# Attention and two mixing layers on one core: batch 0's queries and keys as whole tokens, and one table of priorities for all work

## The chip, the cores and the metric

The kernel runs on one core of a Trainium2 chip. The metric is the device time in microseconds of one execution; the median of three runs is given. A core has TensorE (PE in the profile; its weight loads are PEld), VectorE (DVE), ScalarE (ACT), GpSimd (POOL) and the queue that issues most transfers, SyncE (SP). Each engine works through its own instructions in the order in which they stand in its queue, and a semaphore holds an instruction until what it reads is there.

## The reference, cut to what matters

```python
B, H, S, D = 4, 8, 576, 64                     # queries, keys, values
scores = scale * q @ k^T                       # heads 0-3: the 32 keys up to the query
                                               # heads 4-7: every 4th key, 32 of them
attn = softmax(where(mask, scores, -1e9)); x = attn @ v      # -> (B, S, 512)
xk, xr = x_prev + mu_k * (x - x_prev), x_prev + mu_r * (x - x_prev)   # x_prev: the token before
kk = relu(xk @ w_k) ** 2                       # 512 -> 1024
x = sigmoid(xr @ w_r) * (kk @ w_v)             # MoE 1; 1024 -> 512
h = relu(x @ w_in); u, v = halves of h         # 512 -> 1024
x = (u * (w_spatial @ layernorm(v) + b)) @ w_out             # MoE 2
```

The weights arrive as float64, everything else as float32.

## The kernel before

**Products.** Every large product is made of two 12-bit parts of each operand (names end in `h` and `l`), hi·hi + hi·lo + lo·hi, so a product of 128 rows costs three matmuls of 288 or 512 columns. The parts of activations are made by a cast (ACT or DVE) and a subtraction of two SBUF tiles (DVE or POOL): `xh`/`xl` of the mixed tokens `xm`, `kh`/`kl` of the squared relu `kr`, `x2h`/`x2l` and `gh`/`gl` in MoE 2.

**Weights.** `split_weight` takes 512 float64 columns of 128 rows at a time (a chunk): a transfer into `room`, a scaled copy on ACT into `temps`, a shift and two two-input bit operations on DVE (TENSOR_SCALAR and two SCALAR_TENSOR_TENSOR on `temps`), then the cast to the high part (`wkh`, `wrh`, `wvh`) and the subtraction for the low part (`wkl`, `wrl`, `wvl`, on POOL or DVE). `w_k`, `w_r` and `w_v` are 20 chunks, all before batch 0's first half is through; `w_in` and `w_out` are 12 more (`raw`, `tmp`).

**Attention.** `att(b, qd)` does four heads of a batch: scores of blocks of 32 queries against windows of 64 keys (`psS`), softmax (`mx`, `sm` in the tile `st`, `pr`), transposes (`psT`, `pt`), values (`vw`), and the result into the batch's tokens `x`. Batches 1 to 3 get their queries and keys turned by DVE (`ld` to `qT`, `kT`). Batch 0 has tiles `nat` with 8 tokens to a partition, 72 partitions; TensorE transposes them in pieces of 72 by 128 (`nat_turn`), and ACT and DVE copy halves of 64 partitions into `qT` and `kT`, four copies a tile.

**Halves.** MoE 1 runs per half of a batch's tokens (288): `moe1_k` (products with `w_k`), `moe1_r` (`w_r`, sigmoid), `moe1_v` (`w_v`, and on DVE the gate `x<-psM,x`, four per half, the last step of a half). MoE 2 runs per batch after all of MoE 1.

**Order.** The kernel writes all steps into a `Plan` with what each reads and writes, estimated costs per engine, and a time at which it should stand; `schedule` is a list schedule that gives each step an engine and a place. `order` runs it with the written times as priorities, then twice with due times worked out backward from TensorE's order (`due`), and keeps the order whose estimated end is soonest. Where a step can run on several engines, it takes the one with the soonest estimated end, with a handicap `pen = {'dve': 792, 'pool': 22, 'act': 0}` for all steps alike. Where the plan sees TensorE idle early on, it puts in products of constants that nothing reads (`psT<-const` in the profile). Every planned instruction is recorded on one helper line (L299), so the rows below are told apart by their tiles.

Of the kernel before, what the change touches and what calls it, by code (L numbers as in the profile page):

```python
# [30 lines left out]
CH = 512  # weights converted at a time  # L31
NT = S // P  # full tiles of tokens
# [4 lines left out]
def blocks(dil):  # L37
    """a head's blocks: the first query and the first key of each, two by two, with tokens in
    the order of the head's residue classes; the last of a class repeats 16 queries of the
    one before"""  # L40
    if not dil:
        return [(QB * i, max(0, QB * (i - 1))) for i in range(S // QB)]
    q0, k0 = (0, 32, 64, 96, 112), (0, 0, 32, 64, 80)
    return [
        (CL * c + q0[s], CL * c + k0[s])
        for two, last in (((0, 1), (0, 2)), ((2, 3), (1, 3)))
        for c, s in [(c, s) for c in range(DIL) for s in two] + [(c, 4) for c in last]
    ]


class Plan:
    """Instructions as a program that names what it reads and writes, put in an order in which
    the engines wait little: a list schedule with estimated costs (in ns)."""
# [3 lines left out]
    def __init__(self):  # L57
        self.ops = []
        self.written = {}
        self.read = {}  # L60
        self.turn = {}
        self.groups = {}
        self.hot = {}
        self.end = {}
        self.slow = {}
        self.at = 0.0
# [5 lines left out]
    def add(self, cost, emit, r=(), w=(), table=None, lat=130, at=None, after=(), hot=1.0):  # L72
        i = len(self.ops)
        self.hot[i] = hot
# [19 lines left out]
    def schedule(self, prio):  # L94
        ops = self.ops
        pen = {'dve': 792, 'pool': 22, 'act': 0}
# [30 lines left out]

        def release(i):
            if not ops[i][0]:
                # a step that no engine takes  # L130
# [17 lines left out]
        while any(avail.values()):  # L148
            best = None
            for e, c in avail.items():  # L150
# [4 lines left out]
                for i in sorted((i for i in c if at[i] <= t0 + wide), key=lambda i: (prio[i], i)):  # L155
                    start = max(free[e], at[i])
                    end = start + ops[i][0][e]
                    # another engine that would end it sooner
                    if any(
                        max(free[f], at[i]) + k + pen.get(f, 0) < end + pen.get(e, 0)  # L160
# [8 lines left out]
            if best is None:  # L169
                # each engine leaves its first to another: take the soonest end  # L170
                best = min(
                    (max(free[e], at[i]) + ops[i][0][e], max(free[e], at[i]), i, e)
# [16 lines left out]
            end = start + cost[e] * slow  # L189
# [20 lines left out]
    def due(self, out):  # L210
        """the latest starts with which the tensor engine would never wait, in its order of out"""
        ops = self.ops
        late = [math.inf] * len(ops)
        t = 3000.0
        for _, i, e in out:
            if e == "pe":
                late[i] = t
                t += ops[i][0][e]
        for _, i, e in reversed(out):
            cost, _, deps, _, lat, at, _ = ops[i]  # L220
            if late[i] == math.inf:
                late[i] = 1e9 + at
            for d in deps:
                c = ops[d][0]
                lat = ops[d][4]
                k = min(c.values()) if c else 0
                if "dma" in c:
                    k, lat = c["dma"], 2000
                late[d] = min(late[d], late[i] - lat - k)
        return late  # L230

    def order(self):
        ops = self.ops
        prio = [o[5] for o in ops]
        best = self.schedule(prio) + (prio,)
        guess, out = best[:2]
        for _ in range(2):
            late = self.due(out)
            guess, out = self.schedule(late)
            if guess < best[0]:  # L240
                best = guess, out, late
        if guess > best[0]:
            self.schedule(best[2])
        self.out = best[1]
        # where the tensor engine would idle early on, products that nothing reads keep its clock up
# [24 lines left out]

def act(n):
# [19 lines left out]
class Ordered:  # L291
    """An engine whose instructions keep the order in which they are given."""
# [18 lines left out]
def kernel(  # L311
# [36 lines left out]
    # ---- pools; those of a phase are opened when the plan comes to it  # L348
# [18 lines left out]
    enter("pro", "nat")  # L367
# [4 lines left out]
    # ---- constants  # L372
# [3 lines left out]
    # which keys a block's queries see, a row of blocks: as dilated heads start, as others do  # L376
# [15 lines left out]
    # the room of later batches' tokens serves the conversion of weights first  # L392
# [5 lines left out]
    # ---- weights: float64 words from DRAM, as float32, split into two parts of 12 bits  # L398
    weights = {}

    def split_weight(pool_name, src, rows, cols, name, raw_of, nraw, tmp_of, ntmp, order, step=0, lead=0):
        s = src.bitcast(U32).rearrange("(r p) c -> p r c", p=P)

        def parts():
            if name not in weights:
                weights[name] = (
# [5 lines left out]
        base_at = plan.at  # L412
        for j, (c0, r) in enumerate((c0, r) for c0 in range(0, cols, CH) for r in range(rows)):
# [10 lines left out]
            def words(kr=kr):  # L424
# [3 lines left out]
            add({"dma": 1460}, load, w=[rk], r=order, lat=2000, at=plan.at - lead)  # L428
# [3 lines left out]
            add(  # L432
                {"act": act(CH)},
# [16 lines left out]
            def lower(e, kt=kt, words=words):  # L450
# [5 lines left out]
            add({"dve": dve2(CH)}, shift, r=[tk], w=[tk])  # L456
            add({"dve": dve(CH)}, upper, r=[tk, rk], w=[tk])
            add({"dve": dve(CH)}, lower, r=[tk, rk], w=[tk])
# [3 lines left out]
                r=[tk], w=[(key, 0)],  # L462
# [6 lines left out]
                r=[tk, (key, 0)], w=[(key, 1)],  # L469
            )  # L470

    def wkeys(name, r, c):
# [3 lines left out]
    # ---- batch 0's queries and keys come with 8 tokens to a partition  # L476
    NP = 72
    TP = S // NP
    apart = [0, 0]  # heads of a pair side by side
    nats = [  # L480
        [
            get("nat", [NP, TP, 2, D] if apart[g // 2] else [NP, 2, TP, D], F32, f"nat{x}{g}")
            for g in range(4)
        ]
# [3 lines left out]
    def nat_load(g, at):  # L488
        for x, src in enumerate((q, k)):
            if apart[g // 2]:  # L490
                for h in range(2):
                    dma(
                        820, nats[x][g][:, :, h],
                        src[0, 2 * g + h].rearrange("(i t) d -> i t d", i=NP),
                        w=[("nat", x, g, h)], at=at,
                    )
            else:
                dma(
                    820, nats[x][g],
                    src[0, 2 * g : 2 * g + 2].rearrange("h (i t) d -> i h t d", i=NP),  # L500
                    w=[("nat", x, g, h) for h in range(2)], at=at,
                )
# [971 lines left out]
```

## Time and profile before

| | |
|---|---|
| median of 3 runs | 620.29 us (619.29 to 623.86) |
| profiled execution, first to last instruction | 618.7 us |
| TensorE busy | 566.7 us, mean granted clock 0.958 |
| DVE busy | 309.5 us |
| ACT busy | 311.7 us |
| POOL busy | 274.0 us |

The profile's span is 1.6 us under the median, so what is added or taken in the span is added or taken from the median alike. Busy times are sums over the whole span; the stages differ a great deal, and a busy TensorE can be one that runs at half clock or that multiplies constants.

### The profile page before, as it was taken

The numbers are of one execution on the slowest core, as the hardware profiler recorded it, in microseconds if no ns is written. First come the engines' busy times: TensorE is split into PE (matmuls) and PEld (weight loads), VectorE is DVE, ScalarE is ACT, GpSimd is POOL, SyncE is SP. The second block draws the span as 40 slices with busy tenths as digits, with TensorE's granted clock in tenths as the row PEclk, the third lists the DMA queues.
The fourth block names the chain that finished last, engine by engine and source line by source line (L and its number), as shares of the span: only waits on it lengthen the run. The fifth ranks groups of instructions, "written<-read, shape, count | busy, mean of one in ns | idle before, by whom it ended". The sixth has DMA issues, their size and how long they took to land.

```text
span 618.7 us, 12888 instructions
## 1 busy us (share of the span) xinstructions
PE 566.7 (92%) x5233; PEld 523.4 (85%) x5234; DVE 309.5 (50%) x543; ACT 311.7 (50%) x721; POOL 274.0 (44%) x303
## 2 busy tenths in 40 slices
PE   6766967999799998998899999999999999999996
PEld 4655856889798988988899999987979988998995
DVE  2599999976526169189350500259613314223120
ACT  6575684586285478473453526057335234423321
POOL 3146766573454157166461515008803722551170
PEclk7789788999899999998899999999999999999999
DMA  8998948366123502223200000042010011001002
GB/s 167 184 205 207 226 128 194 79 111 121 22 63 64 116 2 70 88 68 98 78 2 1 2 0 24 1 122 69 1 69 1 1 58 28 1 17 52 2 1 85
DMA packets 91371, 43.75 MB, mean 71 GB/s; under 512 B 76672, under 2 KB 82864, under 8 KB 91312
## 3 DMA queue, kind: packets, MB, share of 16 engines
q1 hardware_dynamic: 90976, 42.09, 28.5%
q0 software_dynamic: 336, 0.84, 0.8%
q8 instruction: 41, 0.67, 0.5%
q14 instruction: 18, 0.15, 0.1%
HBM read 38.20 MB, written 4.72 MB: 69 GB/s over the span
## 4 chain that ended last, share of the span: by engine, by line
PE 61%; DVE 20%; DMA 8%; issue 3%; ACT 3%; POOL 2%; SPq 1%; DVEq 0%; ACTq 0%; POOLq 0%
PE psM L299 44%; PE psB L299 15%; DVE temps L299 4%; DVE tmp L299 3%; DVE xm L299 3%; DVE st L299 3%; PE psT L299 2%; DMA nat<-in_q_dram 2%; DMA room<-in_moe_w_k_dram 2%; DVE pr L299 1%; SPq L299 1%; DVE xl L299 1%; DMA ld<-in_q_dram 1%; POOL pr L299 1%; DMA room<-in_moe_w_r_dram 1%
## 5 line engine op out<-in xcount | busy, mean ns | idle before, releaser
L299 PE MATMUL psM<-kh,wvh 128*128 128x288 f32 x256 | 79.3, 310 | 5.8 <-DVE x L299 3.6
L299 PE MATMUL psM<-xh,wkh 128*128 128x288 f32 x256 | 79.0, 309 | 4.8 <-ACT xh L299 2.3
L299 PE MATMUL psM<-xl,wkh 128*128 128x288 f32 x256 | 78.0, 305 | 1.2 <-POOL xl L299 1.2
L299 PE MATMUL psM<-kh,wvl 128*128 128x288 f32 x256 | 77.1, 301 | 1.3 <-DVE wvl L299 1.1
L299 PE MATMUL psM<-xh,wkl 128*128 128x288 f32 x256 | 77.4, 302 | 0.0
L299 PE MATMUL psM<-kl,wvh 128*128 128x288 f32 x256 | 76.6, 299 | 0.0
L299 POOL TENSOR_TENSOR kl<-kr,kh 128x288 fp32r<-128x288 f32 x55 | 48.5, 884 | 62.5 <-ACT kh L299 61.8
L299 PEld LDWEIGHTS psM<-kh,wvh 128*128 128x128 f32 x256 | 49.7, 194 | 7.9 <-DVE x L299 4.1
L299 PEld LDWEIGHTS psM<-xh,wkh 128*128 128x128 f32 x256 | 50.1, 196 | 5.8 <-ACT xh L299 2.4
L299 POOL TENSOR_TENSOR pr<-pr,st 128x384 f32<-128x384 f32 (+1 forms) x35 | 33.9, 980 | 47.1 <-DVE st L299 45.1
L299 POOL TENSOR_TENSOR xl<-xm,xh 128x288 fp32r<-128x288 f32 x50 | 44.2, 892 | 21.6 <-ACT xh L299 21.4
L299 DVE SCALAR_TENSOR_TENSOR xm<-xd,mu,x 128x288 f32<-128x288 f32 x64 | 47.9, 761 | 9.8 <-POOL xl L299 9.6
L299 PEld LDWEIGHTS psM<-xl,wkh 128*128 128x128 f32 x256 | 50.1, 196 | 1.6 <-POOL xl L299 1.4
L299 PEld LDWEIGHTS psM<-kh,wvl 128*128 128x128 f32 x256 | 49.6, 194 | 1.8 <-DVE wvl L299 1.3
L299 PEld LDWEIGHTS psM<-xh,wkl 128*128 128x128 f32 x256 | 50.3, 197 | 0.0
L299 PEld LDWEIGHTS psM<-kl,wvh 128*128 128x128 f32 x256 | 49.7, 194 | 0.0
L299 ACT ACTIVATE kr<-psM 128x288 f32<-128x288 f32 x64 | 26.1, 408 | 39.9 <-PE psM L299 37.7
L299 PE MATMUL psM<-xh,wrh 128*128 128x288 f32 x128 | 39.6, 309 | 5.5 <-ACT kr L299 3.9
L299 POOL TENSOR_TENSOR vl<-vt,vh 128x512 fp32r<-128x512 f32 x13 | 17.2, 1323 | 52.2 <-ACT vh L299 41.1
L299 DVE TENSOR_TENSOR x<-psM,x 128x288 f32<-128x288 f32 x32 | 14.2, 452 | 52.0 <-PE psM L299 52.0
L299 PE MATMUL psM<-wsh,vh 128*128 128x288 f32 x128 | 38.3, 299 | 1.0 <-ACT u L299 0.5
L299 PE MATMUL psM<-xl,wrh 128*128 128x288 f32 x128 | 38.2, 298 | 0.8 <-POOL xl L299 0.8
(156 smaller groups left out, 1601.0 us busy)
## 6 DMA issues: line engine op xcount, KB each, us to landing
vw<-in_v_dram SPq DMA_DIRECT2D x45, 128.0 KB, 4.1
room<-in_moe_w_k_dram SPq DMA_DIRECT2D x8, 512.0 KB, 8.8
room<-in_moe_w_v_dram SPq DMA_DIRECT2D x8, 512.0 KB
raw<-in_moe_w_in_dram SPq DMA_DIRECT2D x8, 512.0 KB, 3.7
out_dram<-ot SPq DMA_DIRECT2D x16, 256.0 KB, 3.0
ld<-in_q_dram SPq DMA_DIRECT2D x48, 72.0 KB, 2.9
ld<-in_k_dram SPq DMA_DIRECT2D x48, 72.0 KB, 2.5
room<-in_moe_w_r_dram SPq DMA_DIRECT2D x4, 512.0 KB, 6.5
```

What stands on the lines that cost most here:

```text
L299: return self.tc.keep_in_program_order(getattr(self.engine, name)(*args, **kw))
```

## The change

**Batch 0's queries and keys.** The tiles `nat` become views of two large tiles `early0` (queries) and `early1` (keys) that stand where the two parts of `w_v` will stand (pool `w1`, tags `wv0`, `wv1`); the parts of `w_v` are written only after the step `wv room`, that is after all that reads the early tiles. Of heads 0 to 3 a pair comes as 128 partitions of 9 whole tokens, of heads 4 to 7 each head as 48 partitions of 12. `nat_turn` uses ordinary float32 products with the identity, one per token and head (64 by 64 or 48), 168 in all in place of 64 transposes, and two copies of 128 partitions a tile in place of four of 64. Values of heads 4 to 7 of batch 0 lie in the early tiles too, and all values of batch 0 are issued by SP, none by POOL. Two of three score chunks of batch 0 use a `psM` bank. The working tiles of MoE 1 (`mp`) no longer take the place of `nat`.

**Priorities.** `due` and the search for the best of three orders are gone. Each step's priority is its written time plus two numbers of a table `TUNE` (an offset and a slope over the group's steps), and each group has its own handicaps for DVE and POOL. Estimated costs are new (`pe`, `packets`, additions for ACT), and the schedule lets a two-input or wide DVE step and a POOL step slow each other (`begin`, `until`).

```diff
+TUNE = {
+    ('k', 0, 0): {'kh': (-1112, -2225, 400, 22), 'kl': (-5930, 4753, 1500, -800), 'kr': (9298, 2270, -200, 0), 'psM': (1385, 1749, 792, 22), 'xd': (998, -581, 0, 2000), 'xh': (-11122, 10184, 400, 22), 'xl': (-274, 6549, -200, 300), 'xm': (-15869, -4890, 792, 22)},
...
+            more, grow, dve_, pool_ = TUNE.get(g[0], {}).get(g[1], (0, 0, 792, 22))
+            prio.append(o[5] + more + grow * (k / count[g]))
+            self.pens.append({"dve": dve_, "pool": pool_})
...
-        pen = {'dve': 792, 'pool': 22, 'act': 0}
+        pens = self.pens
...
+        def until(e, i, t, c):
+            if e == "pool":
+                h, rate = held["dve"], 0.4
+            elif e == "dve" and two[i]:
+                h, rate = held["pool"], 0.35
+            else:
+                return t + c
+            if h <= t:
+                return t + c
+            return t + c / rate if c / rate <= h - t else h + c - (h - t) * rate
...
-        best = self.schedule(prio) + (prio,)
...
-        for _ in range(2):
-            late = self.due(out)
-            guess, out = self.schedule(late)
...
+        _, self.out = self.schedule(self.tuned())
...
+    early = [
+        pools["w1"].tile([P, NF * DM], F32, tag=f"wv{x}", name=f"early{x}") for x in range(2)
+    ]
...
-                for m in range(4):
-                    if apart[hp // 2]:
-                        i = t[:, 4 * b + m].rearrange("p h d -> p (h d)")
-                    else:
-                        i = t[:, b, 2 * m : 2 * m + 2].rearrange("p t d -> p (t d)")
-                    nc.tensor.transpose(ps[:, m * NP : (m + 1) * NP], i, ident[:NP, :NP])
...
+                for j, tok in enumerate(toks):
+                    for h in range(2):
+                        r = slice(h * D, h * D + m)
+                        nc.tensor.matmul(
+                            ps[h * D : (h + 1) * D, j * m : (j + 1) * m], t[r, tok], ident[r, r],
+                            start=True, stop=True,
+                        )
...
-                choice = {"dma": cost, "pool": 1100} if b == 0 else {"dma": cost}
...
+                dma(cost, o, i, w=[key], at=at1 - 1950 + 40 * qd if b == 0 else at1 - 472)
...
+            if b == 0 and ch != 1:
+
+                ps, skey = bank()
...
+    add({}, lambda e: None, w=["wv room"], after=users_of(early_keys), lat=0)
```

How this moves instructions shows best at three places.

**TensorE at the start**, before: between the turning of the second pair's keys (`nat11`) and the first scores stands the turning of the third pair's queries (`nat02`).

```order
L299 MATMUL psM1_95<-ident_76,nat11_88 128x72 x4
...
L299 MATMUL psM2_96<-ident_76,nat02_85 128x72 x4
L299 MATMUL psM0_94<-ident_76,nat02_85 128x72 x4
...
L299 LDWEIGHTS identb_77
L299 MATMUL psS0_100<-mask_79,identb_77 128x384
L299 MATMUL psS0_100<-kT0_93,qT0_92 32x64 x2
```

The same place after the change: the first scores (now in `psM2`) follow the second pair's keys (`early1`) with nothing but products of constants between, and the third pair's queries come after them.

```order
L436 MATMUL psM0_88<-ident_76,early1_84 64x64 x10
L436 MATMUL psM1_89<-ident_76,early1_84 64x64 x8
...
L436 LDWEIGHTS identb_77
L436 MATMUL psM2_90<-mask_79,identb_77 128x384
L436 MATMUL psM2_90<-kT0_87,qT0_86 32x64 x2
...
L436 MATMUL psM1_89<-ident_76,early0_83 64x48 x16
```

So the first scores no longer stand behind a tile of heads 4 and 5.

**SP's queue ahead of the first weights**, before (the first chunks of `w_k` are the `room` rows; POOL issues five more loads of values by itself):

```order
L299 DMA nat03_86<-in_q_dram 72x2x512
L299 DMA nat13_90<-in_k_dram 72x2x512
L299 DMA vw0_91<-in_v_dram 64x9x64
L299 DMA vw0_91<-in_v_dram 64x8x64
L299 DMA vw0_91<-in_v_dram 64x2x64
L299 DMA room1_80<-in_moe_w_k_dram 128x1024
L299 DMA room3_81<-in_moe_w_k_dram 128x1024
```

and after:

```order
L436 DMA early0_83<-in_q_dram 48x768 x2
L436 DMA vw0_85<-in_v_dram 64x9x64
L436 DMA vw0_85<-in_v_dram 64x8x64
L436 DMA vw0_85<-in_v_dram 64x9x64
L436 DMA room1_80<-in_moe_w_k_dram 128x1024
L436 DMA vw0_85<-in_v_dram 64x8x64
L436 DMA vw0_85<-in_v_dram 64x2x64
L436 DMA early1_84<-in_k_dram 48x768
L436 DMA room3_81<-in_moe_w_k_dram 128x1024
```

The first chunk moved ahead of the last pair's keys and of the values that POOL issued before; the second chunk stands behind four more loads.

**The low parts in batch 0's second half**, before, on POOL:

```order
L299 TENSOR_TENSOR kl1_922<-kr0_877,kh1_912 128x288
L299 TENSOR_TENSOR xd1_638<-x1_1349 128x288
L299 TENSOR_TENSOR kl2_948<-kr1_884,kh2_936 128x288
L299 TENSOR_TENSOR xd2_778<-x1_1349 128x288
L299 TENSOR_TENSOR xd3_810<-x1_1349 128x288
L299 TENSOR_TENSOR kl3_1000<-kr2_905,kh3_987 128x288
L299 TENSOR_TENSOR kl4_1022<-kr0_877,kh4_998 128x288
```

The same steps after the change stand on DVE:

```order
L436 TENSOR_TENSOR kl0_926<-kr2_914,kh0_903 128x288
L436 TENSOR_TENSOR kl1_946<-kr0_877,kh1_929 128x288
L436 TENSOR_TENSOR kl2_959<-kr1_908,kh2_934 128x288
L436 TENSOR_TENSOR kl3_971<-kr2_914,kh3_961 128x288
L436 TENSOR_TENSOR kl4_1030<-kr0_877,kh4_991 128x288
L436 TENSOR_TENSOR kl5_1071<-kr1_908,kh5_1018 128x288
L436 CAST xh2_821<-xm0_746 128x288
L436 TENSOR_TENSOR kl6_1105<-kr2_914,kh6_1093 128x288
L436 SCALAR_TENSOR_TENSOR xm0_746<-xd0_683,mu_78,x1_1432 128x288
```

All eight of this half moved to DVE, in front of the next batch's `xm`. Over the whole program `kl` goes from 55 on POOL and 9 on DVE to 19 and 45, `gl` from 30 and 2 to 0 and 32, and ACT gives 16 of 64 first relus, 16 of 58 casts to `xh` and 12 of 63 casts to `kh` to DVE.

## Rows read from the trace of the kernel before

**Rows 1.** The page: busy us and share of each engine; granted clock in 40 slices.

```profile
PE 566.7 (92%) x5233; PEld 523.4 (85%) x5234; DVE 309.5 (50%) x543; ACT 311.7 (50%) x721; POOL 274.0 (44%) x303
...
PEclk7789788999899999998899999999999999999999
```

**Rows 2.** Windows: width; busy of PE, PEld, DVE, ACT, POOL; clock; DMA share; GB/s.

```profile
0.00:30.00 30.00, 20.81 (x260) 15.64 (x260) 11.38 (x24) 18.89 (x54) 7.22 (x16) 0.72 0.90 177
30.00:120.00 90.00, 67.58 (x975) 59.12 (x974) 88.02 (x135) 57.38 (x128) 56.33 (x53) 0.89 0.77 177
120.00:300.00 180.00, 167.98 (x2020) 159.75 (x2018) 108.61 (x190) 108.28 (x243) 87.25 (x99) 0.98 0.33 76
300.00:400.00 100.00, 97.90 (x724) 97.39 (x724) 25.95 (x44) 43.21 (x111) 36.96 (x45) 0.98 0.04 11
400.00:440.00 40.00, 38.47 (x225) 34.19 (x224) 29.62 (x59) 23.30 (x52) 18.09 (x17) 0.96 0.25 74
440.00:600.00 160.00, 160.00 (x982) 146.44 (x981) 45.48 (x94) 56.52 (x128) 65.73 (x73) 1.00 0.06 22
```

**Rows 3.** The chain that ended last: shares by engine; its longest piece.

```profile
PE 61%; DVE 20%; DMA 8%; issue 3%; ACT 3%; POOL 2%; SPq 1%; DVEq 0%; ACTq 0%; POOLq 0%
...
302.52 93.12 PE psM L299 x690
```

**Rows 4.** Timeline of the first 30 us: start, us, what, and what ended idling.

```profile
6.03 9.29 SPq L299 DMA_DIRECT2D vw<-in_v_dram  x3
...
12.71 2.03 ACT L299 COPY kT<-psM 64x288 f32<-64x288 f32 x3
15.37 1.23 SPq L299 DMA_DIRECT2D room<-in_moe_w_k_dram  x2
...
16.36 1.19 PE L299 MATMUL psM<-ident,nat 72*128 72x72 f32 x8 [3.05 <-DMA nat<-in_q_dram]
...
18.37 1.51 PE L299 MATMUL psS<-kT,qT 64*32 64x64 f32 x48
...
25.27 0.67 ACT L299 ACTIVATE temps<-room 128x512 f32<-128x512 f32 x1 [0.81 <-DMA room<-in_moe_w_k_dram]
```

**Rows 5.** Groups of DVE from 30 to 120 us: busy us, mean ns of one.

```profile
L299 DVE SCALAR_TENSOR_TENSOR temps<-room,temps 128x512 uint32<-128x512 uint32 x38 | 37.1, 995 | 0.0
L299 DVE TENSOR_SCALAR temps<-temps 128x512 uint32<-128x512 uint32 x19 | 13.0, 692 | 0.9 <-ACT temps L299 0.9
L299 DVE SCALAR_TENSOR_TENSOR xm<-xd,mu,x 128x288 f32<-128x288 f32 x12 | 10.4, 883 | 0.0
L299 DVE TENSOR_TENSOR xl<-xm,xh 128x288 fp32r<-128x288 f32 x3 | 2.7, 901 | 0.0
```

**Rows 6.** The tiles temps, kl: duration ns min/median/max; single DVE steps while POOL is idle.

```profile
L299 DVE SCALAR_TENSOR_TENSOR temps<-room,temps x40: 641/765/1775, 27.2 to 110.8; 128x512 uint32<-128x512 uint32 x40
L299 DVE TENSOR_SCALAR temps<-temps x20: 385/421/1515, 26.0 to 108.7; 128x512 uint32<-128x512 uint32 x20
...
L299 POOL TENSOR_TENSOR kl<-kr,kh x55: 797/809/1267, 67.4 to 378.7; 128x288 fp32r<-128x288 f32 x55
L299 DVE TENSOR_TENSOR kl<-kr,kh x9: 448/902/1541, 78.6 to 375.5; 128x288 fp32r<-128x288 f32 x9
...
27.20 0.68 DVE L299 SCALAR_TENSOR_TENSOR temps<-room,temps 128x512 uint32<-128x512 uint32 x1
...
117.03 0.50 DVE L299 SCALAR_TENSOR_TENSOR xm<-xd,mu,x 128x288 f32<-128x288 f32 x1
```

**Rows 7.** Timeline of DVE: the 4th and the 20th of the 32 gates.

```profile
120.43 0.41 DVE L299 TENSOR_TENSOR x<-psM,x 128x288 f32<-128x288 f32 x1
...
299.47 0.45 DVE L299 TENSOR_TENSOR x<-psM,x 128x288 f32<-128x288 f32 x1
```

**Rows 8.** Waits, whole span (DVE) and 120 to 320 us (PE): total us, times, longest.

```profile
DVE kl L299 <- ACT kh L299: 56.9, 5, 13.1
...
PE psM L299 <- DVE x L299: 4.2, 2, 3.6
PE psT L299 <- POOL pr L299: 2.1, 5, 1.0
```

**Rows 9.** Timeline of ACT: attention's last results of batch 0; the first cast of w_v.

```profile
58.62 0.67 ACT L299 COPY x<-psT 128x256 f32<-128x256 f32 x2
...
90.85 0.62 ACT L299 CAST wvh<-temps 128x512 fp32r<-128x512 f32 x1
```

More of the change, by code (lines that the diff above doesn't have):

```diff
@@ L65, in __init__ @@
         self.slow = {}
+        self.two = []
+        self.tags = []
+        self.tag = ("start",)
         self.at = 0.0
@@ L70, in slot, with add @@
         return self.turn[name]
-    def add(self, cost, emit, r=(), w=(), table=None, lat=130, at=None, after=(), hot=1.0):
+    def add(self, cost, emit, r=(), w=(), table=None, lat=130, at=None, after=(), hot=1.0, two=False):
         i = len(self.ops)
+        self.two.append(two)
+        self.tags.append(self.tag)
         self.hot[i] = hot
@@ L126, in schedule, with begin @@
         out = []
+        held = {"dve": 0.0, "pool": 0.0}
+        two = self.two
+        def begin(e, i):
+            t = max(free[e], at[i])
+            if e == "dve" and two[i] == "both":
+                t = max(t, held["pool"])
+            return t
+        def until(e, i, t, c):
[8 more added lines that the diff above has]
+            return t + c / rate if c / rate <= h - t else h + c - (h - t) * rate
         def release(i):
@@ L188, in schedule @@
                 table[0] = tab
-            end = start + cost[e] * slow
+            end = until(e, i, start, cost[e] * slow)
+            if e == "pool" or e == "dve" and two[i]:
+                held[e] = end
             for f in cost:
@@ L268, in order, with pe, packets @@
         return res
+def pe(n, cols):
+    return n * (4.7 + cols * 0.442)
+def packets(n, size):
+    took = {128: 13, 256: 23, 512: 30, 1024: 58, 1920: 125, 2048: 112, 2304: 133, 3072: 165, 4096: 219}
+    return n * took[size] / 16
 def act(n):
@@ L399, with split_weight @@
     weights = {}
-    def split_weight(pool_name, src, rows, cols, name, raw_of, nraw, tmp_of, ntmp, order, step=0, lead=0):
+    def split_weight(pool_name, src, rows, cols, name, raw_of, nraw, tmp_of, ntmp, order, step=0, lead=0, room=()):
         s = src.bitcast(U32).rearrange("(r p) c -> p r c", p=P)
@@ L405, in parts @@
             if name not in weights:
+                if name == "wv":
+                    weights[name] = tuple(
+                        pools[pool_name].tile([P, rows, cols], F32R, tag=f"wv{x}", name=f"wv{x}")
+                        for x in range(2)
+                    )
+                    return weights[name]
                 weights[name] = (
@@ L474, in wkeys, with spread, cut @@
         return [((name, r, c0), 0), ((name, r, c0), 1)]
-    NP = 72
-    TP = S // NP
-    apart = [0, 0]
+    def spread(hp):
+        return 9 if hp < 2 else 12
+    NATS = sum(spread(g) for g in range(4)) * D
+    VW = 2 * 10 * D
+    early = [
+        pools["w1"].tile([P, NF * DM], F32, tag=f"wv{x}", name=f"early{x}") for x in range(2)
+    ]
+    def cut(t, n, c0):
+        return t[:, c0 : c0 + n * D].rearrange("p (t d) -> p t d", d=D)
     nats = [
[L481 to L484, printed above, removed]
+        [cut(early[x], spread(g), D * sum(spread(i) for i in range(g))) for g in range(4)]
         for x in range(2)
@@ L550 @@
+            w_ = len(toks) * m
+            add(
+                {"act": actp(w_) + 147, "dve": dve(w_) + 100}, keep, r=[pkey],
+                w=[key + (2 * b,), key + (2 * b + 1,)],
+            )
     NQK = 3
@@ L740, in att @@
                     ),
-                    r=[s_key, ("mx", pk)], w=[("pr", pk)],
+                    r=[s_key, ("mx", pk)], w=[("pr", pk)], two=not pe_mask,
                 )
@@ L1039, in users_of @@
         return res
-    def open_mp(e):
-        stacks["pro"].close()
-        enter("one", "mp", reuse_waits="tile")
-    add({}, open_mp, w=["mp"], after=users_of([("nat", x, g, h) for x in range(2) for g in range(4) for h in range(2)]), lat=0)
+    plan.at = 1391
+    plan.tag = ("wv room",)
+    add({}, lambda e: None, w=["wv room"], after=users_of(early_keys), lat=0)
+    split_weight("w1", w_v, NF, DM, "wv", lambda i: raws[i], raw1, lambda i: tmps[i], tmp1, [], 51, 480, ["wv room"])
+    plan.at = 600
+    plan.tag = ("start",)
+    fresh_x(1, [("raw", 0), ("raw", 2)])
+    fresh_x(2, [("tmp", i) for i in range(4)])
+    fresh_x(3, [("raw", 1), ("raw", 3)])
     gap = [361, 786, 488]
@@ L1369, in moe2 @@
                 lambda e, eg=eg, g=g: copy(e, eg()[:, :, b % 2], f32(g()[:, :, NT * P :])),
-                r=[(nm, c, 1) for c in range(NC)], w=[("e" + nm, b % 2)],
+                r=[(nm, c, 1) for c in range(NC)], w=[("e" + nm, b % 2)], two="both",
             )
```

268 lines of the change are left out of this document (146 added, 122 removed), and 84 rows, old and new, of the table TUNE.

## The prediction, on record before the run

> **What bounds the kernel now.** I read the page first, then the busy times by stretch, then the chain of waits, then single rows in the stretches where TensorE stands. The page shows TensorE busy for 92% of the span [rows 1]. That number misleads early on. In the first 120 us TensorE is busy 20.8 + 67.6 = 88.4 us, but at granted clocks of 0.72 and 0.89 (a mean between the full level and the half one), and part of that multiplies constants [rows 2]. From 440 to 600 us it is busy 160.00 of 160.00 at full clock: nothing that the change does to other engines can shorten that. The chain's longest piece, 93.12 us for 690 products, is 135 ns a product and ends at 395.6 [rows 3]; it is bound by TensorE alone.
>
> So the time to be won lies ahead of 440 us. From 0 to 30 us the transfers run at a share of 0.90 and 177 GB/s, and DVE is busy 11.38 us [rows 2]. From 30 to 120 us DVE is busy 88.02 of 90.00 us: this is the stage of the 20 weight chunks, and DVE sets its pace. From 120 to 300 us TensorE idles 180.00 - 167.98 = 12.0 us and loses another 180 x (1 - 0.98) = 3.6 us to the clock; from 300 to 440 us it idles 2.1 + 1.5 us and loses 2.0 + 1.6 us to the clock [rows 2]. Beyond 120 us that is 15.6 + 7.2 = 22.8 us in all, the most that better order can return there.
>
> **The start.** The first scores run at 18.37 us. The last copy of the second pair's keys ended at 12.71 + 2.03 = 14.74 us, but the turning of `nat02`, which stands before the scores, waited 3.05 us for its transfer and ran at 16.36 [rows 4]. After the change that tile stands behind the scores. Ahead of them are four tiles of 0.295 MB and the mask, 1.43 MB; at 177 GB/s that is 8.1 us, with about 1 us to the first issue 9 us, and with turning and two copies (0.7 us a copy at the pace of the `kT` row, 2.03 / 3) 11 to 12 us. If the tiles come no sooner, the end of the copies still bounds it: 14.7 us. So the scores come 3.7 to 7 us earlier; I take 6. The first chunk of `w_k` was converted from 25.27 us on [rows 4]. Ahead of it and with it stood 0.5 + 2.9 MB on SP and 0.7 MB on POOL, 4.1 MB, 23 us at that rate, which agrees. Now it is 3.3 MB: 18.4 + 1 us, 5 to 6 us earlier. Both inputs of DVE's long queue therefore come some 6 us earlier. The copies themselves fall from four of 64 partitions to two of 128 a tile, which frees ACT for the 18 exponentials of the first block. Turning takes 168 products in place of 64 transposes: 24 products (48 records) of scores took 1.51 us, 63 ns each, so 10.6 us, against 8 transposes in 1.19 us, 149 ns each, 9.5 us [rows 4]. TensorE has that 1 us to spare there. If it had none, it would cost 1 us. I take **-6 us** for the start; ends -3 and -8.
>
> **The new wait.** The casts of `w_v` must now wait until batch 0's attention is through. Its last results of that kind started at 58.62 us, the first cast of `w_v` at 90.85 [rows 9]: 32 us of cover. I cost it at nothing; if attention came later than that, ACT's later casts, and behind them `temps`, would stand for the excess.
>
> **30 to 120 us.** The order of the changed kernel has, in DVE's queue up to the fourth gate, more work: 8 more low parts of weights at 0.68 us, two more steps each of `xd`, `pr`, `mx` and `pt`, fewer `xm`. With the durations that these steps have while POOL is idle (0.68 us for two-input steps of 512, 0.50 for `xm`, 0.45 for differences of 288, 0.42 for the shift) [rows 6] the queue adds up to 86.0 us before and 95.2 after, +9.2. But POOL has 35 steps there in place of 57, 31 us in place of 53 by its own group means. What POOL costs DVE shows in the same stretch: 38 x (995 - 680) + 19 x (692 - 421) + 12 x (883 - 500) + 3 x (901 - 450) ns = 12.0 + 5.1 + 4.6 + 1.4 = 23.1 us lost [rows 5, 6] beside 56.33 us of busy POOL [rows 2], 0.41 us of DVE for each us of POOL. So 22 us less POOL returns 9.1 us. The sum is **0**; ends -5 and +5, since a single two-input step loses anything from nothing to 1.1 us (641 to 1775 ns) [rows 6].
>
> **120 to 300 us.** From the 4th gate (120.43) to the 20th (299.47) [rows 7] DVE's queue grows by 35.5 us at those durations (95.4 to 130.9: 24 more `kl` at 0.45, 14 squares, 13 `xd`, some 12 casts each to `xh` and `kh`), and POOL's falls by 30 us, which returns 12. Net +23 us, in a stretch in which DVE idles 180.00 - 108.61 = 71 us [rows 2]. It fits, and each step is done sooner: a `kl` takes 0.81 us on POOL and 0.45 on DVE alone [rows 6]. TensorE's waits there are for gates, low parts and softmax steps of POOL [rows 8]. I take half of the 15.6 us: **-8 us**; ends 0 and -13, and above 0 in a rival below. **300 to 440 us**, where `w_in` and the change to MoE 2 stand, I take **-3** of 7.2; ends +2 and -5. **After 440 us**: 0, by the full row.
>
> The sum: 618.7 - 6 + 0 - 8 - 3 = 601.7 us of span. The span stands 1.6 us under the median of 620.29, so **603 us**. The best ends make 618.7 - 8 - 5 - 13 - 5 + 1.6 = 589.
>
> **A rule that would give more.** Rows 5 and 6 show a two-input DVE step at 995 ns on average where it takes 680 alone. As a rival, let each us of POOL that leaves the saturated stretch give DVE a full us back: a DVE step would then stand still for as long as POOL's runs. Up to the fourth gate that is -22 + 9.2 = -13 us in place of 0, so 590 us. For it speaks the row's maximum of 1775 ns, 1.1 us over the step alone. Against it speaks the mean of 0.41. I give it 0.15. The Trainium skill, SBUF — State Buffer, section "Who interferes with whom", says that a DVE instruction with two SBUF inputs and a GpSimd instruction that reads SBUF exclude each other for a whole instruction; this case's rows show the loss, but only 0.41 of POOL's time, because many DVE steps there do not lose at all.
>
> **Rivals that give less.** First, no change: the whole tokens come no sooner than DVE can use them. The transfers still run at a share of 0.77 up to 120 us and 0.90 before 30, the weights pace the stage, and the fourth gate stays within 3 us of 120. In the middle the waits for POOL turn into waits for DVE, whose queue is 23 us fuller. Then -3 and 0 to -3 remain: 613 to 619, say 616. Chance 0.17. That the priorities do not do what they say (an order worked out from estimated costs that the chip does not keep) ends here too.
>
> Second, **slower**: the low parts block DVE. An engine works in order, so a `kl` on DVE that waits for ACT's `kh` holds all that is behind it. Before, five such waits cost DVE 56.9 us, the longest 13.1 [rows 8], without harm, because POOL did the rest. After the change 45 of 64 `kl` and all `gl` are on DVE, and in batch 0's second half all eight stand in a row in front of the next batch's `xm`. If the next half's `xm` and softmax steps lie behind them, TensorE waits at the end of each half. At some 6 us for each of five halves (half of the longest wait) that is +30 us, against -6 - 3 of the other terms: 618.7 + 21 + 1.6 = 641; with two such halves 623. It decides from the point where these waits lose more than 17 us to TensorE. Against it: DVE keeps 71 - 23 = 48 us of idle time there to absorb waits. Chance 0.11.
>
> **How the numbers follow.** The forecast (-17 us) has 0.57, the bigger gain 0.15, no change 0.17, slower 0.11. The likeliest gives 603 us. The range runs from 589, rounded down to 588 (the best ends, and most of the bigger gain), to 620 (all of the no-change case); it leaves out the slow case and the lower part of the bigger gain, less than 2 in 10. Within 1% is within 6.2 us, which is about what a measurement of this kernel can tell from no change, so faster means under 614. The forecast and the bigger gain lie there, with a little of the no-change case: 0.57 + 0.15 + 0.01. Same takes 0.16, slower 0.11.
>
> **What would show it.** In the changed profile the first scores should run at 11 to 13 us and the first conversion of `w_k` at about 19 to 20. The fourth gate should stand near 114 us, with DVE full from 24 us on, and its mean for `temps` steps under 995 ns. The 20th gate should stand near 285, with DVE busy some 130 us between the two gates and TensorE idle 4 to 8 us. Once MoE 2 is under way nothing should differ. The forecast is wrong if the fourth gate stays near 120 (the stage is paced by transfers or by DVE's contents), if waits of TensorE for `xm`, `xl` or gates grow after 120 us (DVE has become the bound), or if the change to MoE 2 lengthens by more than 2 us because its low parts now stand on DVE.

## The result, and the profile after

The changed kernel takes **602.46 us** (median of 4 runs, 600.81 to 603.41) against 620.18 us (619.29 to 623.86) of the kernel before: a ratio of 0.9703, 95% interval 0.9672 to 0.9734. In a later series of runs it took 603.04 against 619.51 us (0.9741, 0.9707 to 0.9775). The forecast was 603, with 588 to 620 around it. The profiled execution has a span of 599.0 us in place of 618.7.

The page, busy time and granted clock, against [rows 1]:

```profile
PE 567.9 (95%) x5515; PEld 524.5 (88%) x5516; DVE 385.1 (64%) x789; ACT 260.9 (44%) x590; POOL 147.3 (25%) x168
...
PEclk9775998999999999999999999999999999999999
```

Busy times by stretch, columns as in [rows 2], first by the clock of the program, then from gate to gate:

```profile
0.00:30.00 30.00, 26.09 (x552) 21.41 (x556) 16.51 (x35) 14.54 (x52) 1.04 (x8) 0.85 1.04 215
30.00:120.00 90.00, 73.27 (x1057) 64.86 (x1052) 88.90 (x155) 57.63 (x124) 41.59 (x41) 0.86 0.84 169
120.00:300.00 180.00, 174.59 (x2043) 166.05 (x2038) 134.81 (x283) 92.19 (x197) 50.29 (x61) 1.00 0.32 73
300.00:400.00 100.00, 99.53 (x729) 97.29 (x728) 47.90 (x107) 33.12 (x78) 16.96 (x20) 1.00 0.09 24
400.00:440.00 40.00, 40.00 (x226) 35.06 (x225) 34.15 (x76) 16.58 (x37) 9.65 (x9) 1.00 0.13 46
...
0.00:113.63 113.63, 92.99 (x1511) 80.48 (x1513) 99.08 (x177) 67.34 (x164) 40.91 (x48) 0.85 0.90 182
113.63:284.41 170.78, 165.53 (x2011) 156.64 (x2010) 126.08 (x270) 83.80 (x175) 46.13 (x56) 1.00 0.33 71
```

The same two stretches of the kernel before, to its 4th gate and from there to its 20th:

```profile
0.00:120.43 120.43, 88.82 (x1235) 75.19 (x1237) 99.83 (x158) 76.55 (x181) 63.98 (x70) 0.84 0.80 176
120.43:299.47 179.04, 167.53 (x2015) 159.29 (x2013) 107.65 (x188) 107.87 (x243) 86.50 (x97) 0.98 0.33 76
```

Read them in pairs. Up to the 4th gate DVE is busy for the same time in both (99.08 and 99.83 us), but within 113.63 in place of 120.43 us: its idle time fell from 20.6 to 14.6. Of these 6.0 us 5.1 lie in the first 30 us, where DVE is busy 16.51 us in place of 11.38 [rows 2]. Between the gates DVE does 18 us more and TensorE idles 5.25 us in place of 11.5, and its clock is 1.00 in place of 0.98. Behind the 20th gate 314.6 us are left in place of 319.2.

The two gates, the first scores, the first conversion of `w_k` and the groups of DVE from 30 to 120 us, in the timeline and the groups of the changed kernel, against [rows 4, 5, 7]:

```profile
10.77 0.86 PE L436 MATMUL psM<-kT,qT 64*32 64x64 f32 x45
...
23.24 0.67 ACT L436 ACTIVATE temps<-room 128x512 f32<-128x512 f32 x1
...
113.63 0.45 DVE L436 TENSOR_TENSOR x<-psM,x 128x288 f32<-128x288 f32 x1
...
284.41 0.46 DVE L436 TENSOR_TENSOR x<-psM,x 128x288 f32<-128x288 f32 x1 [0.50 <-PE psM L436]
```

```profile
L436 DVE SCALAR_TENSOR_TENSOR temps<-room,temps 128x512 uint32<-128x512 uint32 x36 | 31.6, 884 | 0.1
L436 DVE TENSOR_SCALAR temps<-temps 128x512 uint32<-128x512 uint32 x18 | 12.0, 669 | 0.0
L436 DVE SCALAR_TENSOR_TENSOR xm<-xd,mu,x 128x288 f32<-128x288 f32 x15 | 9.5, 657 | 0.6 <-DMA mu<-in_moe_mu_k_dram 0.5
```

DVE's waits for `kh`, 56.9 us in 5 before [rows 8], are 11.3 us in 14:

```profile
DVE kl L436 <- ACT kh L436: 11.3, 14, 2.7
```

One caution for all that follows: the changed kernel's second profile has its 4th gate at 116.78 and its 20th at 286.72. The start differs by 3 us from one execution to the next; the stretch between the gates (170.78 and 169.94) by less than 1. So stretches behind the 4th gate are compared from gate to gate, and at the start only differences above 3 us count. Of the kernel before there is one profile, so the spread of its 179.04 us between the gates is not known.

Three of the experiments below leave the orders of DVE, ACT and POOL up to the 4th gate as they are, and so add executions of the start. These are their 4th gates: two with the start of the kernel before (`j_before_kl_on_dve`, `l_gate_ahead`), one with the start of the changed kernel (`i_old_engines`), and the changed kernel's second profile:

```profile
122.70 0.41 DVE L299 TENSOR_TENSOR x<-psM,x 128x288 f32<-128x288 f32 x1
120.98 0.41 DVE L299 TENSOR_TENSOR x<-psM,x 128x288 f32<-128x288 f32 x1
113.28 0.45 DVE L437 TENSOR_TENSOR x<-psM,x 128x288 f32<-128x288 f32 x1
116.78 0.45 DVE L436 TENSOR_TENSOR x<-psM,x 128x288 f32<-128x288 f32 x1
```

With 120.43 and 113.63 that is three of each: 120.4 to 122.7 before, 113.3 to 116.8 after, and a mean of 6.8 us between them.

### The profile page after: what moved, and what is told of

Its sections match the earlier page's. It is cut to its first block, busy times and chain, and to the rows that moved or that the text cites. A ratio compares the mean times of both kernels' runs of the same rounds, so it can differ in the third digit from the quotient of the medians.

```text
span 599.0 us, 13366 instructions
## 1 busy us (share of the span) xinstructions
PE 567.9 (95%) x5515; PEld 524.5 (88%) x5516; DVE 385.1 (64%) x789; ACT 260.9 (44%) x590; POOL 147.3 (25%) x168
## 4 chain that ended last, share of the span: by engine, by line
PE 72%; DVE 11%; DMA 7%; ACT 4%; issue 2%; SPq 2%; POOL 1%; DVEq 0%; ACTq 0%; POOLq 0%
PE psM L436 51%; PE psB L436 17%; PE psT L436 3%; DVE temps L436 3%; DMA ld<-in_q_dram 2%; DMA room<-in_moe_w_k_dram 2%; SPq L436 2%; DVE st L436 2%; DMA room<-in_moe_w_r_dram 2%; DVE qT L436 1%; DVE pr L436 1%; DVE xm L436 1%; DMA mu<-in_moe_mu_k_dram 1%; PE psS L436 1%; ACT temps L436 1%
## 5 line engine op out<-in xcount | busy, mean ns | idle before, releaser
L436 PE MATMUL psM<-kh,wv 128*128 128x288 f32 x512 | 110.9, 301 | 3.4 <-ACT x L436 3.1
L436 PEld LDWEIGHTS psM<-kh,wv 128*128 128x128 f32 x512 | 85.1, 191 | 5.3 <-ACT x L436 3.8
L436 PE MATMUL psM<-kl,wv 128*128 128x288 f32 x256 | 76.1, 297 | 0.0
L436 PEld LDWEIGHTS psM<-kl,wv 128*128 128x128 f32 x256 | 48.9, 191 | 0.0
L436 PE MATMUL psM<-x2h,wih 128*128 128x288 f32 x128 | 38.0, 297 | 0.3 <-DVE x2h L436 0.3
L436 PE MATMUL psM<-x2l,wih 128*128 128x288 f32 x128 | 37.8, 296 | 0.2 <-DVE x2l L436 0.2
L436 PE MATMUL psM<-x2h,wil 128*128 128x288 f32 x128 | 37.8, 295 | 0.0
L436 PE MATMUL psM<-xh,wrl 128*128 128x288 f32 x128 | 37.8, 295 | 0.0
L436 PE MATMUL psM<-wsl,vh 128*128 128x288 f32 x128 | 37.7, 295 | 0.0
L436 PE MATMUL psM<-wsh,vl 128*128 128x288 f32 x128 | 37.6, 294 | 0.0
```

The source lines that it names most:

```text
L436: return self.tc.keep_in_program_order(getattr(self.engine, name)(*args, **kw))
```

## The experiments

**The two halves of the change alone.** First the new start with the planner, the costs and the handicaps of the kernel before:

```
-        _, self.out = self.schedule(self.tuned())
+        (search over due times, one set of handicaps, no contention, costs as before)
```

> The changed kernel's whole-token start and its room, but the old planner: old costs, old handicaps, no contention, no table. Theory (start worth -6 us by DVE's earlier inputs, the rest by the new order): first scores at 11 to 12 us, 4th gate near 114, from the 4th to the 20th gate 176 to 180 us, in all 612 to 616 us. Rival 'the start is nearly all': 603 to 606 us. Rival 'the new order is all': 618 to 622 us, with the 4th gate within 2 us of 120.

Measured: 626.54 us, ratio 1.0101 (1.0047 to 1.0155). The first scores run at 9.03 us and the first conversion at 20.69, both earlier than in the full change, but the 4th gate stands at 129.2. None of the three expectations holds, and the start alone gives no gain. From the 4th to the 20th gate the run takes 175.35 us, 3.7 less than the kernel before, with the old planner. Waits up to 130 us, first of DVE, then of ACT:

```profile
DVE temps L312 <- ACT temps L312: 10.2, 3, 7.7
...
DVE qT L312 <- DMA ld<-in_q_dram: 6.0, 1, 6.0
...
ACT temps L312 <- DMA room<-in_moe_w_k_dram: 20.2, 6, 8.0
```

The same row of ACT is 2.2 us in the full change and 6.0 in the kernel before. The old planner puts ten loads of values ahead of the first chunk of `w_k` in SP's queue (three in the full change) and eight loads of the next batch's tokens ahead of the second, and a transposing that waits for those tokens in front of DVE's first chunk.

Then the new planner, costs and table with the tokens as before:

```
-        nats = [cut(early[x], ...)]     # whole tokens, in w_v's room
+        nats = [get("nat", [72, 2, 8, 64], ...)]     # as before, with a room of their own
```

> The new planner, costs and table, but batch 0's queries and keys as before: 72 partitions, 64 transposes, copies of 64 partitions, room of their own (the table's entries for those loads and turnings are left out). Theory: 4th gate at 117 to 121 us, from the 4th to the 20th 170 to 173 us as in the changed kernel, 606 to 611 us. Rival 'the tokens are all': 616 to 620 us. Rival 'the tokens are nothing, the order brings the start too': 601 to 604 us with the 4th gate near 114.

Measured: 639.84 us, ratio 1.0310 (1.0265 to 1.0356), the first product of `w_k` at 87.3 us, the 4th gate at 142.2 and 182.1 us from there to the 20th. None of its three expectations holds either. The table of priorities was made for other loads, which may be why; no run shows it. Both halves lose alone, so a time of each cannot be told from them; what they say is that the gain of the start came only with both together.

**Is it DVE's wait for the next batch's tokens?** The first half again, with that wait out of the way:

```
+    behind(lds[8:16], loads[5])     # the next batch's loads, behind w_k's sixth chunk
+    behind(lds[:8], loads[3])       # and behind its fourth
+    (the first two transposings stand behind three chunks' steps)
```

> The run with whole tokens and the old planner, in which DVE stood 6.0 us for the next batch's tokens at 23 us and 7.7 us for a chunk of w_k at 47 us. Here those loads, eight and eight, stand behind the fourth and the sixth chunk of w_k in SP's queue, and the first two transposings behind three chunks' steps on DVE. Theory (the early start is worth its 6 us only if DVE's queue does not stand afterwards): 4th gate at 115 to 121 in place of 129.2 us, 612 to 619 us in all. Rival 'whole tokens give nothing with the old order': 4th gate above 126 us, 623 to 627 us.

Measured: 629.46 us, ratio 1.0181 (1.0130 to 1.0233), 4th gate 132.5. The wait for tokens fell to 2.3 us, but ACT's waits for `w_k` are 20.3 us as before the edit. The theory falls: the wait was not what held the stage, the late weights remain, and by which loads ahead of them is left open.

**What POOL costs DVE.** In the changed kernel 37 steps of POOL up to the 4th gate run on DVE, in place:

```
+        (i, "dve" if n < stop and e == "pool" and plan.two[i] else e)
```

> The changed kernel; 37 two-input steps of POOL that stand ahead of the 4th gate run on DVE, at the same place in the order. Alone they take 19 us on DVE and some 35 us on POOL. Theory (0.41 us of DVE lost for each us of POOL): DVE +19 - 14 = +5 us, 4th gate near 118, 606 to 609 us. Rival 'DVE stands still for as long as POOL runs': -35 + 19 = -16 us, 4th gate near 98, 586 to 590 us. Rival 'POOL costs DVE nothing': +19 us, 4th gate near 132, 619 to 623 us.

Measured: 602.22 us, ratio 0.9716 (0.9663 to 0.9770), 4th gate 115.8, within the spread of the start. The busy times of 30 to 120 us and DVE's groups there:

```profile
30.00:120.00 90.00, 74.29 (x1037) 64.46 (x1036) 87.95 (x189) 57.16 (x124) 0.32 (x3) 0.85 0.81 165
```

```profile
L437 DVE SCALAR_TENSOR_TENSOR temps<-room,temps 128x512 uint32<-128x512 uint32 x36 | 24.1, 675 | 0.1
L437 DVE TENSOR_SCALAR temps<-temps 128x512 uint32<-128x512 uint32 x18 | 7.4, 414 | 0.0
L437 DVE SCALAR_TENSOR_TENSOR xm<-xd,mu,x 128x288 f32<-128x288 f32 x13 | 6.4, 507 | 0.0
```

Without POOL the steps fall to 675, 414 and 507 ns from 884, 669 and 657: 36 x 209 + 18 x 255 + 15 x 150 ns = 7.5 + 4.6 + 2.3 = 14.4 us for 41.3 us of POOL that are gone, 0.35 us each. The 37 steps cost DVE 19 us, and these three groups show three quarters of that paid back. Over all steps that DVE has in both kernels up to the 4th gate, 15.5 us come back for the 19.2 that are added, so 3.7 us should be left over. The time lies below the 606 to 609 us of my theory: what is left over does not show beside the start's spread. Neither "a full us for each us of POOL" (98 us for the gate) nor "nothing" (132) is near.

**Engine or order, between the gates.** The changed kernel with its 45 `kl` on POOL in place of DVE:

```
+        (i, "pool" if e == "dve" and plan.kinds[i][1] == "kl" else e)
```

> The changed kernel; the 45 low parts kl that DVE makes are made by POOL, at the same place in the order. POOL gets 45 x 0.81 = 36 us more, DVE 20 us less. Theory (the middle's gain comes from steps that are done sooner on DVE): from the 4th to the 20th gate 175 to 179 in place of 171 us, 606 to 611 us. Rival 'the gain is in the order, not in the engine': within 2 us of the changed kernel. Rival 'kl on DVE holds up what is behind it': 2 to 6 us faster than the changed kernel.

Measured: 605.69 us, ratio 0.9762 (0.9713 to 0.9810); 172.2 us from the 4th to the 20th gate, 317.3 from there to the end of the span. Of the stretch's gain of 8 us 1.4 to 2.2 go, not most of it: my theory misses its 175 to 179. The median is 2.7 to 3.2 us above the changed kernel's two, so the rival's "within 2 us" is missed as well: the engine counts, but for the smaller part.

From the 4th to the 32nd gate, in the new order, eight kinds of steps on the engines that did most of them before:

```
+        if kind in ("kl", "xd") or kind == "pr" and plan.two[i]:
+            return "pool" if "pool" in cost else e
+        if kind in ("kr", "kh", "xh", "x", "pt"):
+            return "act" if "act" in cost else e
```

> The changed kernel's order kept, but between the 4th and the 32nd gate the steps go back to the engines that did most of them before: kl, xd and the softmax scaling to POOL, relus, squares, casts to kh and xh and copies to ACT (156 steps leave DVE). Theory (the middle's gain comes from steps done sooner on DVE): from the 4th to the 20th gate 177 to 180 us in place of 171, 610 to 616 us in all. Rival 'the gain lies in the order': 171 to 174 us between the gates, 602 to 606 us.

Measured: 606.27 us, ratio 0.9797 (0.9747 to 0.9847). From the 4th to the 20th gate:

```profile
113.28:286.05 172.77, 165.29 (x2011) 156.63 (x2010) 84.75 (x155) 107.72 (x243) 82.48 (x103) 1.00 0.32 70
```

DVE is busy 84.75 us there, less than the 107.65 before the change, and still the stretch takes 172.77 us, 2 to 3 more than in the changed kernel and 6.3 less than before. What is longer lies ahead of the 5th gate: TensorE waits there 3.17 us for ACT's `x`, 1.34 in the changed kernel.

```profile
144.67 0.40 PE L437 MATMUL psM<-kh,wv 128*128 128x288 f32 x1 [3.17 <-ACT x L437]
...
142.30 0.40 PE L436 MATMUL psM<-kh,wv 128*128 128x288 f32 x1 [1.34 <-ACT x L436]
```

So most of the gain is in the order, as the rival said; its time of 602 to 606 is just exceeded, and the profile is of the fastest of the four runs. The new planner's order is not the only one that is shorter: with whole tokens and the old planner the stretch took 175.35 us. Conversely, the kernel before with 48 `kl` on DVE, order kept:

```
+        (i, "dve" if n > gates[3] and plan.ops[i][6][0][0] == "kl" else e)
```

> The kernel before, with its order; from the 4th gate on the 48 low parts kl that POOL makes are made by DVE, at the same place in the order. DVE gets 48 x 0.45 = 22 us more, POOL 39 us less. Theory (sooner on DVE): 3 to 6 us faster than the kernel before, from the 4th to the 20th gate 174 to 177 in place of 179 us. Rival 'order': within 2 us of it. Rival 'a waiting kl holds up DVE's queue': 3 to 10 us slower, with waits of DVE for kh above 20 us.

Measured: 618.06 us, ratio 0.9965 (0.9938 to 0.9992); 174.9 us between the gates in its profile, 4.1 less than before, as my theory has it; the median is 1.9 us lower (0.5 to 3.8 by the interval), as the rival "order" has it. The profile does not settle it, because in it TensorE's wait for the 5th gate is shorter and the clock stays at 1.00 up to the 20th gate:

```profile
160.31 0.40 PE L299 MATMUL psM<-kh,wvh 128*128 128x288 f32 x1 [1.65 <-DVE x L299]
```

The kernel before waits 3.56 us at that place, as shown next. DVE's waits for `kh` are 52.2 us in 35, the longest 5.2, and do no harm: the "slower" rival's mechanism is there and finds idle time.

**What the order does.** In the kernel before, TensorE's longest wait in the stretch has a clear cause. Timeline, first DVE, then TensorE:

```profile
150.76 0.78 DVE L299 STREAM_TRANSPOSE qT<-ld 128x576 f32<-128x576 f32 x1 [4.77 <-DMA ld<-in_q_dram]
...
158.69 0.45 DVE L299 TENSOR_TENSOR x<-psM,x 128x288 f32<-128x288 f32 x1
...
159.19 0.40 PE L299 MATMUL psM<-kh,wvh 128*128 128x288 f32 x1 [3.56 <-DVE x L299]
```

A transposing of the next batch's queries waits 4.77 us for its transfer. Behind it in DVE's order stands the 5th gate, which frees the bank that TensorE waits for. And in the windows the granted clock is 1.00 up to 160, where TensorE is busy 6.44 of 10 us, and 0.83 in the 10 us behind it, a mean between the full level of 2.4 GHz and the half one of 1.2; it is 0.83 again from 280 and from 300 on:

```profile
150.00:160.00 10.00, 6.44 (x49) 6.21 (x48) 9.03 (x18) 3.24 (x6) 5.88 (x7) 1.00 0.51 83
160.00:170.00 10.00, 9.93 (x90) 9.57 (x90) 3.84 (x8) 2.41 (x6) 2.33 (x3) 0.83 0.01 2
270.00:280.00 10.00, 8.59 (x63) 8.12 (x62) 8.98 (x13) 6.16 (x16) 6.17 (x6) 1.00 0.16 52
280.00:290.00 10.00, 8.25 (x51) 8.01 (x50) 9.93 (x15) 4.41 (x10) 6.24 (x6) 0.83 0.31 107
300.00:310.00 10.00, 8.12 (x48) 7.89 (x49) 1.50 (x1) 6.14 (x15) 5.45 (x6) 0.83 0.22 60
```

The wait and the clock behind it make 3.56 + 10 x 0.17 = 5.3 us. So in the kernel before only the two transposings were moved behind that gate:

```
+    todo[gate + 1 : gate + 1] = moved     # qT and kT of the next pair, and the loads that take their room
```

> The kernel before, with one pair of DVE's steps in another place: the two transposings of the next batch's tokens that stood ahead of the fifth gate at 151 to 155 us (the first waited 4.77 us there for its transfer) stand behind that gate, and the eight loads that take their room with them. Theory (the middle's loss before came from single waits in DVE's order, each followed by a lower clock): TensorE's wait of 3.56 us at 159 and the stretch at 0.83 behind it go, 8th gate 3.5 to 5 us earlier, 615 to 617 us. Rival 'the wait only moves': within 1.5 us of the kernel before. Rival 'the scores come later and TensorE waits for them': 621 to 624 us.

Measured: 615.02 us, ratio 0.9936 (0.9906 to 0.9966), 4.5 us under the kernel before, with 2.1 to 5.8 as the interval's ends. The wait and the low clock at 160 are gone:

```profile
150.00:160.00 10.00, 10.00 (x78) 10.00 (x77) 8.33 (x16) 3.79 (x7) 6.60 (x8) 1.00 0.33 54
160.00:170.00 10.00, 9.96 (x103) 9.59 (x102) 0.46 (x1) 5.51 (x13) 1.62 (x2) 1.00 0.43 96
```

From there on every gate stands earlier (the 8th 162.18 for 166.97, the 31st 391.04 for 395.73), and the 4.7 us are kept to the end of the span (614.0). From the 4th to the 20th gate it takes 173.75 us, 5.3 less than before. One place in DVE's order is worth more than half of the 8.3 us that the whole change wins between the gates. The changed kernel has no such wait there: its last transposings ahead of the 5th gate run at 133.49 and 134.52 us without waiting, and the gate itself waits for TensorE:

```profile
146.63 0.46 DVE L436 TENSOR_TENSOR x<-psM,x 128x288 f32<-128x288 f32 x1 [1.68 <-PE psM L436]
```

**The start, in small steps.** In the changed kernel the first two conversions of `w_k` ahead of the second and third block's exponentials, and the first chunk's DVE steps with them:

```
+    ahead([conv[0]] + steps[:3], third_maximum)
+    ahead([conv[1]], exps[2])
```

> The changed kernel; the first two conversions of w_k on ACT stand ahead of the second and the third block's exponentials, and the first chunk's three DVE steps ahead of the third maximum. Theory (DVE's queue sets the 4th gate, so what it gets done before it is full comes off): first conversion at 18 to 19 us, 1.8 us of DVE's work moves into idle time, 4th gate at 111 to 112.5, 600 to 601.5 us. Rival 'the transfers pace the stage': 4th gate within 0.6 us of 113.6, 602 to 603 us. Rival 'the exponentials come later and TensorE with them': 603 to 605 us.

Measured: 601.39 us, ratio 0.9697 (0.9651 to 0.9744); first conversion at 17.13, 4th gate 112.2. The gate and the time are what my theory gives, but the profile is of the fastest of the four runs, and both lie inside the spread of the start, so it is not shown. The same, with the loads of `w_k` one place earlier and a second chunk:

```
+    for o, n in zip(loads[1:6], spots): todo[n] = o
+    todo.insert(todo.index(v0), loads[0])
+    ahead([conv[1]] + steps[3:6], third_maximum)
```

> The changed kernel; the first six loads of w_k each stand one place earlier among the loads, the first ahead of batch 0's values, and the first two chunks' conversions and DVE steps stand in the gaps ahead of the second and the third maximum. Theory (what DVE gets done before it is full comes off the time): first conversion at 13 to 15 us, some 3.6 us of DVE's work in idle time, 4th gate at 110 to 111.5, 598 to 600 us. Rival 'from there the transfers pace DVE': 4th gate at 112 to 113.6, 600 to 602.5 us. Rival 'values and scores come late': above 603 us.

Measured: 604.71 us (604.13 to 605.62), ratio 0.9775 (0.9743 to 0.9807), against 603.04 (0.9741, 0.9707 to 0.9775) of the changed kernel on the same chip. Conversions at 14.82 and 19.53, but the third at 31.84 (31.81 in the changed kernel there), and the 4th gate at 117.7. The theory falls: DVE is not busier in the first 30 us (16.39 us, 16.41 in the changed kernel there) and by then has done no more of the chunks (4.20 and 4.18 us), and the runs are some 2 us slower. Which rival holds is open. The time lies where the third one, "values and scores come late", has it. That the transfers pace DVE from there on is not shown: from 30 to 120 us DVE is busy 85.5 us, 85.7 in the changed kernel there, and in both its longest wait is for ACT's `pt`; the third conversion stands behind a copy that waits 1.40 us for TensorE:

```profile
30.78 1.22 ACT L437 COPY kT<-psM 128x384 f32<-128x384 f32 x2 [1.40 <-PE psM L437]
31.84 0.66 ACT L437 ACTIVATE temps<-room 128x512 f32<-128x512 f32 x1
```

The two loads of `mu` 40 us earlier, since the first `xm` waits for them:

```
+    todo[at:at] = early_mu     # right behind the tokens of batch 0
```

> The changed kernel; the two loads of mu stand in SP's queue right after the tokens of batch 0, some 40 us earlier. The first xm then no longer waits for mu. Theory (DVE is full there and has other work): 0 to -1 us, the first k product up to 1 us earlier. Rival 'the first k product waits for mu, and TensorE with it': the first k product at 47 to 50 in place of 53.9 us and 599 to 601 us in all. Rival 'the small packets hold up the weights': 603 to 604 us.

Measured: 604.46 us (602.62 to 606.75), ratio 0.9753 (0.9710 to 0.9796). The first `xm` waits for nothing, yet the first conversion slips to 26.63 and the 4th gate to 119.4 in the profile, which is of the slowest of the four runs; the medians say 1 to 2 us slower, and the ranges overlap. That is the direction of the third rival; its cause is not shown. There is no gain, at least.

The changed kernel again, for the spread:

> The changed kernel once more, beside the others on the same chip: 600 to 604 us; the spread of its runs says which differences of 1 to 3 us can be told.

Measured: 603.04 us (600.94 to 604.05). No kernel tried beats it by more than that spread.

## Why the prediction was right, step by step

**What bounds the kernel** was read rightly: DVE up to the 4th gate, single waits and the clock up to 440 us, nothing behind. If only products whose results are used are counted, each at the distance between starts that its kind has at full clock, both kernels hold some 518 us of them; from the 350th us of this work on (446 us before, 426 after) the changed kernel is 19.4 to 20.1 us ahead of the one before, all the way to the end.

**The start, -6.** Measured -6.8 in one profile and -3.6 in the other, and -6.8 in the mean of three each. The size is right and DVE's idle time is where it came from; the way there was not. The first scores run at 10.77, 7.6 us earlier; the transfers moved 215 GB/s in the first 30 us, not the 177 that were taken. But the first conversion comes only 2 us earlier. The transfers were not what it waited for: it runs at 23.24, not 19 to 20, because ACT first does 12 exponentials and two copies; its transfer had landed at 18.0. What DVE gained ahead of 30 us (busy 16.51 for 11.38) is steps of the weight chunks, 2.0 us, softmax work of batch 0, 1.4, copies of queries and keys, 1.0, and one more clearing of `pt`, 0.9. And I gave the whole term to the tokens: the run with the tokens alone has earlier scores than the change and a later gate. So the new order is part of it; that it is the order of loads, with `w_k` between the values, is likely from ACT's waits (20.2 and 2.2 us) and not shown. The right size of this term is in part luck.

**The new wait, 0.** Right: ACT idled 1.16 us ahead of the first cast of `w_v` at 80.78, and what ended that was DVE's `temps`, not the room.

**30 to 120 us, 0.** Right in both halves: DVE busy up to the gate within 0.8 us of before, and 0.35 us of DVE for each us of POOL in the three groups, 0.38 over all of DVE's steps up to the gate (15.5 us for 40.9), where the prediction took 0.41 from the means of [rows 5, 6].

**120 to 300 us, -8.** Measured 170.78 for 179.04, -8.3, and DVE busy 126 where 130 was forecast, TensorE idle 5.25 in the range of 4 to 8. The reason given, steps done sooner on DVE, is worth 2 to 3 us of it: with the old engines the stretch is 172.77. The rest is order: the wait behind the transposing and the low clock after it alone are 4.7 to 5.3. Here the mechanism was named wrongly, and the size was right because it was taken as a half of the visible loss and not worked out from the mechanism: that it fits is luck.

**300 to 440, -3.** Measured -4.6 from the 20th gate to the end. The runs say to which half it belongs: behind the 20th gate the four other runs with the old planner have 318.9 to 320.4 us left, the ones with whole tokens among them, and those with the new one 313.8 to 317.3, the one without whole tokens 313.8. So it came with the new order, not with the tokens; by which step was not tried. **After 440, 0.** Right, within 0.7 us by the same count.

**The rivals.** "A full us of DVE for each us of POOL" is excluded by the run without POOL. "Slower" did not come: 11.3 us of waits for `kh`. "No change" is excluded by the interval.

## What to carry to other kernels

Where a whole schedule changes, read the in-order engines for the instruction that waits for a transfer, and look what stands behind it: one pair of transposings in front of one gate was worth 4.7 us, because TensorE stood 3.6 us and then ran at a lower clock. Here the engine on which a step runs counted for less than its place. And test the halves of a change alone before giving either a price: each half of this one alone was slower than the kernel before.

## What the runs showed of the hardware

A wait of TensorE can cost more than its length: with 6.44 of 10 us busy at 150 to 160 in the kernel before, the next 10 us ran at 0.83, another 1.7 us. It does not do so each time. In the run with the old engines TensorE waited 3.17 us and was busy 6.83 of 10 us, and the clock stayed at 1.00:

```profile
140.00:150.00 10.00, 6.83 (x52) 6.59 (x51) 4.72 (x9) 3.32 (x6) 5.78 (x8) 1.00 0.13 20
150.00:160.00 10.00, 10.00 (x77) 10.00 (x77) 1.31 (x3) 2.48 (x6) 1.21 (x2) 1.00 0.01 2
```

Between 30 and 120 us DVE lost 0.35 us for each us of busy POOL, in steps with one input too: the shift took 669 ns beside POOL and 414 without.

Two transfers of 2 KB each among the first loads went with a first conversion 3.4 us later and DVE busy 13.20 in place of 16.51 us in the first 30 us; whether the transfers themselves, their place or this slow execution did it was not tried apart.
